# First unit's 47-point result copied across partitions on chip; its row sums on VectorE, its threshold on ACT; token matrix loaded six blocks ahead

## The chip, the cores and the metric

The kernel runs on one core of one Trainium2 chip. The metric is the device time of the program in microseconds, lower is better. The core has five engines that each work through their own list of instructions in order: TensorE (PE, with its weight loads as PEld), VectorE (DVE), ScalarE (ACT), GpSimd (POOL) and SyncE (SP, which here only issues transfers). Transfers are carried out by 16 DMA engines; in this kernel they are issued by SP and by ACT.

## What is computed

```python
def _attn_ref(x, w_r, w_i, b_r, b_i):          # x: 8 x 3008 x 256
    X = np.fft.rfft(x, axis=1)
    Xr, Xi = X.real, X.imag
    Yr = Xr @ w_r - Xi @ w_i + b_r
    Yi = Xr @ w_i + Xi @ w_r + b_i
    Yr = np.sign(Yr) * np.maximum(np.abs(Yr) - 0.01, 0.0)
    Yi = np.sign(Yi) * np.maximum(np.abs(Yi) - 0.01, 0.0)
    return np.fft.irfft(Yr + 1j * Yi, n=3008, axis=1)

def _moe_ref(x, w_tok1, w_tok2, w_ch1, w_ch2):
    h = np.maximum(x.transpose(0, 2, 1) @ w_tok1, 0.0) @ w_tok2
    u = x + h.transpose(0, 2, 1)
    return u + np.maximum(u @ w_ch1, 0.0) @ w_ch2   # 256 -> 1536 -> 256
```

The output is `_moe_ref` of the result of `_attn_ref`. All is float32.

## The kernel before

The transform over 3008 = 47 x 64 points is done with matmuls in two steps: a 47-point step (`dft47`, `stage1`) and a 64-point step (`forward`). The batch of 8 is cut into five units: two of one batch entry (units 0 and 1), three of two. For each unit, `stage1` takes 13 groups of 5 residues each (`NG`, `GS`): a load of `x` with 120 partitions, matmuls with the constant `f1`, an eviction by ACT into a tile `a`, and a store to a scratch tensor `a_d` in DRAM. The next step needs the data with another index on the partitions: it is read back as `a2`, one load for each of 12 pairs `kp` of frequencies. Then, per `kp`: `forward` (matmuls `px`, eviction `xf`, a row sum), `mix` (matmuls `pm` with the channel weights, bias, threshold at 0.01 with DVE), `inverse` (matmuls `pi`, stored to `b_d`), and `tokens` (matmuls `gp` with the transformed token matrix).

Unit 0 is special (`plain`): it runs in `begin`, before anything else can, in float32 without splitting into high and low halves. Beside it, `begin` prepares what all units share. The token matrix `wt1` comes as 13 blocks in float64 words that ACT and DVE turn into float32 (`load_wide`, `narrow`: two ACT and six DVE operations a block); it goes through the 47-point step as well (`prepare_w1`, result in `a_w`), and through a 64-point step (`make_w`). The channel weights `w1` and `w2` are turned into float32 and split.

The loop of `begin` has `NW + KP` passes; in pass n stand one or two groups of `wt1`, `forward` of n, `mix` of n−1, `inverse` of n−3, and from n = `NW` on `make_w` of n−`NW` and `tokens` two passes later. From pass `NC` on the channel weights are prepared (`ahead`). `NC` also decides, before the change, which subtractions of the threshold run on POOL (pairs below 8) and which on DVE. Once `begin` is done, TensorE works through the channel matmuls (`channel`) of one unit while the next unit's transform is woven in.

The order on each engine comes from a scheduler that starts from this program order. Waits follow from the tiles: PSUM has a pool of four banks (`w`) for all matmul results but two. Each DMA counts up one of eight lanes (`DMAHW0` to `DMAHW7`), which are given out in turn to the DMAs of SP and ACT together; a DMA waits until the one before it on its lane has landed. So no more than eight are on their way, and an engine whose next instruction is a DMA stands until that lane is free.

Of the kernel before, what the change touches and what calls it, by code (L numbers as in the profile page):

```python
# [10 lines left out]
F32 = mybir.dt.float32  # L11
# [9 lines left out]
NW, NC = 11, 8  # L21
# [3 lines left out]
GS = 5  # L25
# [93 lines left out]
def tile_kernel(ctx: ExitStack, tc: tile.TileContext, io):  # L119
# [67 lines left out]
    sc = const.tile([128, 16], F32, name="sc")[:, :2]  # L187
# [33 lines left out]
    def sum_diff(x, w, eng, pool):  # L221
        if pool is not None:
            return x
# [10 lines left out]
    def stage1(sd, dst, g, w, pool):  # L234
# [3 lines left out]
        elif dst is a_w:  # L238
            a = pool.tile([120, 2, w], F32, name="a", bufs=2)
        else:  # L240
            t = ("xtl", "xf", "wt", "et", "xtl", "xf", "wt", "et", "xtl")[g % 9]
            a = wk.tile([120, 2, w], F32, tag=t, name="a", bufs=2)
# [11 lines left out]
        rows = dst.rearrange("(i n) k w -> (n k) i w", i=2)  # L254
        (DMA if pool else PUT).dma_start(out=rows[g * 120:g * 120 + n * KH, :, :w], in_=a[:n * KH])

    def dft47(load, dst, w, ahead, eng, pool=None):
# [17 lines left out]
        for g in range(NG):  # L275
# [4 lines left out]
            stage1(sds.pop(g), dst, g, w, pool)  # L280
# [7 lines left out]
    def prepare_w1(pool):  # L288
        tags = ("hl", "o", "early", "hl", "o", "early", "hl", "o", "hl")

        raws = {g: load_raw(io["wt1"][g], 2 * DT, pool) for g in range(3)}

        def load(g):
            return load_wide(io["wt1"][g], 2 * DT, pool, tags[g % 9], raw=raws.pop(g, None)).rearrange("p (i w) -> p i w", i=2)

        return dft47(load, a_w, DT, 3, V, pool)
# [60 lines left out]
    def split_w1(q, t, f):  # L357
        cols = slice(q * 512, (q + 1) * 512)
        split(wc["w1h"][:, t, cols], wc["w1l"][:, t, cols], f, S, V)
# [13 lines left out]
    def parts(u):  # L373
# [6 lines left out]
        def load_unit(g):  # L380
            src = io["x"][bs[0] // 2, g].rearrange("q i (b c) -> q i b c", b=2)
            if plain and g < 12:
                x = wc["x"][g // 6][:, g % 6]
            else:
                x = ld([120, 2, nb, C], "x")
# [11 lines left out]
        def forward(kp, b, a2):  # L397
            pt = bank("px")
            for t in range(2):
                for ab in range(2):  # L400
                    o = (2 * t + ab) * 128
                    PE.matmul(pt[:, o:o + 128], lhsT=a2[:, ab, b, t * 128:(t + 1) * 128], rhs=f2cols(2 * kp + ab), start=True, stop=True)  # L402
            xf = wk.tile([128, 3, 4, 64], F32, tag="xth" if plain else "xf", name="xf", bufs=2)
            S.copy(out=xf[:, 1:3], in_=pt.rearrange("p (q i m) -> p i q m", i=2, m=64))  # L404
            G.tensor_tensor(out=xf[:, 0], in0=xf[:, 1], in1=xf[:, 2], op=ALU.add)  # L405
# [8 lines left out]
        def mix(xt, yh, yl, eng=V):  # L414
# [15 lines left out]
            V.tensor_scalar(out=cl, in0=y, scalar1=LAM, scalar2=-LAM, op0=ALU.min, op1=ALU.max)  # L430
            eng.tensor_tensor(out=yh if plain else y, in0=y, in1=cl, op=ALU.subtract)
# [408 lines left out]
```

## Time and profile before

| | us |
|---|---|
| runs: median (lowest to highest of 3) | 2465.56 (2464.93 to 2467.65) |
| profiled execution, its time | 2465.8 |
| profiled execution, its span | 2464.0 |
| TensorE busy / DVE / ACT / POOL | 2431.6 / 1103.6 / 858.7 / 328.0 |
| first forward matmul (`px`) starts | 42.73 |
| first matmul of the first unit's tokens result (`pu`) starts | 163.88 |

The profile shows one execution. Times in a timeline are microseconds from the start of the span; a row gives the start, the length, the engine, the line of the program, the operation, output <- input, how many, and in brackets how long the engine had been idle and what ended that. `SPq` and `ACTq` are the queues of SP and ACT in which DMAs are issued.

### The profile page before, as it was taken

How to read it: one execution, taken by the hardware profiler on the slowest of the kernel's cores; microseconds unless marked ns; L12 is line 12 of the kernel's file. 1: busy time of each engine (PE TensorE's matmuls, PEld its weight loads, DVE VectorE, ACT ScalarE, POOL GpSimd, SP SyncE). 2: the span in 40 equal slices, each digit the busy share in tenths (PEclk: the TensorE clock that was granted, in tenths of full speed). 3: DMA queues.
4: the chain of work that ended last, by engine and by line, in shares of the span. 5: the costliest groups of instructions: out<-in, count | busy, mean ns of one | idle time of the engine just before them, and what ended most of it. 6: DMA issues, size and time to landing. Idle time of an engine off the chain costs nothing.

```text
span 2464.0 us, 31639 instructions
## 1 busy us (share of the span) xinstructions
PE 2431.6 (99%) x12800; PEld 2116.0 (86%) x12800; DVE 1103.6 (45%) x1734; ACT 858.7 (35%) x1559; POOL 328.0 (13%) x279
## 2 busy tenths in 40 slices
PE   7989999999999999999999999999999999999999
PEld 6768999988888888888888898888888888888887
DVE  5876665455445444433344454434334333232332
ACT  4464444443334343333333343333333222222221
POOL 0200223122223111111111110111111000000000
PEclk9999999999999999999999999999999999999999
DMA  8785334562333453222222363222311122112110
GB/s 250 215 260 155 93 114 140 150 192 84 99 90 97 123 170 91 77 71 88 71 80 80 95 175 105 79 73 82 112 62 41 54 65 63 47 60 78 39 56 18
DMA packets 150484, 252.17 MB, mean 102 GB/s; under 512 B 11009, under 2 KB 104161, under 8 KB 150337
## 3 DMA queue, kind: packets, MB, share of 16 engines
q1 hardware_dynamic: 123825, 199.80, 27.2%
q10 hardware_dynamic: 26512, 50.34, 6.5%
q8 instruction: 101, 1.65, 0.3%
q14 instruction: 46, 0.38, 0.1%
HBM read 162.68 MB, written 87.43 MB: 102 GB/s over the span
## 4 chain that ended last, share of the span: by engine, by line
PE 90%; DMA 3%; issue 3%; DVE 2%; SPq 1%; ACT 0%; POOL 0%; DVEq 0%; ACTq 0%; POOLq 0%
PE ph L178 10%; PE po L179 10%; PE po L178 10%; PE po L180 10%; PE ph L179 10%; PE ph L180 10%; PE pu L679 4%; PE px L402 3%; PE pm L180 2%; PE pm L178 2%; PE pm L179 2%; PE pu L178 2%; PE pu L179 2%; PE pu L180 2%; PE gp L178 2%
## 5 line engine op out<-in xcount | busy, mean ns | idle before, releaser
L718 DVE SCALAR_TENSOR_TENSOR hlo<-ph,hh 128x512 fp32r<-128x512 f32 (+4 forms) x588 | 392.0, 667 | 644.2 <-ACT hh L717 641.3
L717 ACT ACTIVATE hh<-ph 128x512 fp32r<-128x512 f32 (+4 forms) x588 | 340.4, 580 | 816.6 <-PE ph L180 811.5
L178 PE MATMUL ph<-uh,w1h 128*128 128x512 f32 (+4 forms) x1176 | 455.9, 388 | 0.3 <-DVE hlo L718 0.3
L179 PE MATMUL ph<-ul,w1h 128*128 128x512 f32 (+4 forms) x1176 | 449.7, 382 | 0.1
L179 PE MATMUL po<-hlo,w2h 128*128 128x512 f32 (+4 forms) x1176 | 448.2, 381 | 1.6 <-DVE hlo L718 1.6
L180 PE MATMUL ph<-uh,w1l 128*128 128x512 f32 (+4 forms) x1176 | 448.8, 382 | 0.0
L178 PE MATMUL po<-hh,w2h 128*128 128x512 f32 (+4 forms) x1176 | 448.7, 382 | 0.0
L180 PE MATMUL po<-hh,w2l 128*128 128x512 f32 (+4 forms) x1176 | 448.0, 381 | 0.0
L179 PEld LDWEIGHTS po<-hlo,w2h 128*128 128x128 f32 x1176 | 220.9, 188 | 40.7 <-DVE hlo L718 2.3
L180 PEld LDWEIGHTS ph<-uh,w1l 128*128 128x128 f32 x1176 | 221.1, 188 | 39.5
L178 PEld LDWEIGHTS po<-hh,w2h 128*128 128x128 f32 x1176 | 221.0, 188 | 38.6
L180 PEld LDWEIGHTS po<-hh,w2l 128*128 128x128 f32 x1176 | 221.0, 188 | 38.6
L178 PEld LDWEIGHTS ph<-uh,w1h 128*128 128x128 f32 x1176 | 221.5, 188 | 35.6 <-DVE hlo L718 1.2
L179 PEld LDWEIGHTS ph<-ul,w1h 128*128 128x128 f32 x1176 | 221.6, 188 | 34.7 <-DVE ul L688 0.8
L137 DVE TENSOR_TENSOR xtl<-xf,xth 128x768 fp32r<-128x768 f32 x84 | 80.5, 958 | 193.9 <-ACT xth L134 193.7
L405 POOL TENSOR_TENSOR xf<-xf 128x256 f32<-128x256 f32 x96 | 80.7, 841 | 551.3 <-ACT xf L404 550.9
L137 POOL TENSOR_TENSOR yl<-z,yh 128x512 fp32r<-128x512 f32 x72 | 92.7, 1288 | 412.8 <-ACT yh L134 412.8
L178 PE MATMUL pm<-wmh,xth 128*128 128x256 f32 x504 | 144.5, 287 | 0.1
L686 ACT COPY uf<-pu 128x470 f32<-128x470 f32 (+23 forms) x188 | 62.7, 375 | 232.4 <-PE pu L679 232.4
L180 PE MATMUL pm<-wmh,xtl 128*128 128x256 f32 x504 | 142.5, 283 | 0.4 <-DVE xtl L137 0.3
L179 PE MATMUL pm<-wml,xth 128*128 128x256 f32 x504 | 142.4, 283 | 0.0
L679 PEld LDWEIGHTS pu<-g,b 96*128 96x128 f32 x1024 | 130.7, 191 | 3.7 <-issue 0.3
(121 smaller groups left out, 3223.1 us busy)
## 6 DMA issues: line engine op xcount, KB each, us to landing
wt<-wt_d SPq DMA_DIRECT2D x28, 940.0 KB, 5.7
x<-in_x SPq DMA_DIRECT2D x39, 480.0 KB, 4.6
a<-a_d SPq DMA_DIRECT2D x36, 512.0 KB, 3.9
b_d<-bt ACTq DMA_DIRECT2D x36, 512.0 KB, 3.3
out<-o SPq DMA_DIRECT2D x34, 512.0 KB, 2.8
a_d<-a ACTq DMA_DIRECT2D x36, 480.0 KB, 3.5
wt<-wt_d SPq DMA_DIRECT2D x21, 752.0 KB, 5.1
b<-b_d SPq DMA_DIRECT2D x32, 480.0 KB, 6.2
```

The costliest lines, as they stand in the source:

```text
L137: lo_eng.tensor_tensor(out=lo, in0=src, in1=hi.bitcast(F32), op=ALU.subtract)
L178: PE.matmul(out, lhsT=wh, rhs=xh, start=start, stop=False)
L179: PE.matmul(out, lhsT=wh, rhs=xl, start=False, stop=False)
L180: PE.matmul(out, lhsT=wl, rhs=xh, start=False, stop=stop)
L402: PE.matmul(pt[:, o:o + 128], lhsT=a2[:, ab, b, t * 128:(t + 1) * 128], rhs=f2cols(2 * kp + ab), start=True, stop=True)
L405: G.tensor_tensor(out=xf[:, 0], in0=xf[:, 1], in1=xf[:, 2], op=ALU.add)
L679: PE.matmul(pt[:, s * TOKS:(s + 1) * TOKS], lhsT=b2[:, s, cs], rhs=g2[:, 0 if s0 + s == 0 else 1], start=False, stop=s == k - 1)
L686: S.copy(out=ufs[m][:, ct, lo - at:hi - at], in_=pt[:, lo - c0:hi - c0])
L717: S.activation(out=hh, in_=pt, func=AF.Relu)
L718: V.scalar_tensor_tensor(out=hlo, in0=pt, scalar=0.0, in1=hh.bitcast(F32), op0=ALU.max, op1=ALU.subtract)
```

## The change

For unit 0, the DRAM scratch of the 47-point result goes. `a2` is one tile of 128 partitions that holds the whole result (in the place of the later `w1` tile), and each group's eviction is followed by two DMAs from SBUF to SBUF that put 120 rows of 1 KB into 5 partitions of 24 rows each: the cosine half on ACT's queue into partitions from 0 on, the sine half on SP's into partitions from 64 on. `forward` reads `a2` directly.

DVE now adds and subtracts the two halves of each `x` group of unit 0, which halves the matmuls of `stage1` there (two for a group in place of four). The row sum in `forward` of unit 0 moves from POOL to DVE. The threshold of unit 0 becomes relu(y − 0.01) − relu(−y − 0.01): two ACT operations and one subtraction, always on DVE, in place of a DVE minimum and maximum and a subtraction on POOL or DVE. The tiles of `x` for unit 0 take the places of buffers that the narrowing uses later.

The blocks of the token matrix are loaded six ahead (before: three), and narrowed two ahead (before: three). Their stores to `a_w` are issued by ACT (before: SP). `NW` goes from 11 to 8, `NC` from 8 to 12, and every pass takes two groups of the token matrix (before: one and two in turn). The two tiles `w1h` and `w1l` become one, `w1`. The loads of `scale` and `g2` stand ahead of unit 0's groups.

```diff
-NW, NC = 11, 8
+NW, NC = 8, 12
...
-            raw = pool.tile([rows, n, 2], U32, name="raw", bufs=3)
+            raw = pool.tile([rows, n, 2], U32, name="raw", bufs=6)
...
     def sum_diff(x, w, eng, pool):
-        if pool is not None:
+        if pool is not None and w == DT and eng is None:
             return x
...
+                elif not adds:
+                    PE.matmul(pt[:120, o:o + w], lhsT=f1[:, i], rhs=sd[:, i], start=True, stop=True)
                 else:
                     PE.matmul(pt[:120, o:o + w], lhsT=f1[:, i], rhs=sd[:, 0], start=True, stop=False)
                     PE.matmul(pt[:120, o:o + w], lhsT=f1[:, 2 * i], rhs=sd[:, 1], start=False, stop=True)
             S.copy(out=a[:, i0:i0 + each].rearrange("p i w -> p (i w)"), in_=pt[:120])
-        rows = dst.rearrange("(i n) k w -> (n k) i w", i=2)
-        (DMA if pool else PUT).dma_start(out=rows[g * 120:g * 120 + n * KH, :, :w], in_=a[:n * KH])
+        if pool is not None and not adds:
+            for i in range(2):
+                (PUT, DMA)[i].dma_start(out=dst[i * N2 + g * GS:i * N2 + g * GS + n], in_=a[:n * KH, i])
+        else:
+            rows = dst.rearrange("(i n) k w -> (n k) i w", i=2)
+            PUT.dma_start(out=rows[g * 120:g * 120 + n * KH, :, :w], in_=a[:n * KH])
...
-        raws = {g: load_raw(io["wt1"][g], 2 * DT, pool) for g in range(3)}
+        raws = {g: load_raw(io["wt1"][g], 2 * DT, pool) for g in range(6)}
...
+            f = load_wide(None, 2 * DT, pool, tags[g % 9], raw=raws.pop(g)).rearrange("p (i w) -> p i w", i=2)
+            if g + 6 < NG:
+                raws[g + 6] = load_raw(io["wt1"][g + 6], 2 * DT, pool)
+            return f
...
-        return dft47(load, a_w, DT, 3, V, pool)
+        return dft47(load, a_w, DT, 2, None, pool)
...
+                    x = a2[:, 2 * kp + ab, cs] if plain else a2[:, ab, b, cs]
+                    PE.matmul(pt[:, o:o + 128], lhsT=x, rhs=f2cols(2 * kp + ab), start=True, stop=True)
...
-            G.tensor_tensor(out=xf[:, 0], in0=xf[:, 1], in1=xf[:, 2], op=ALU.add)
+            (V if plain else G).tensor_tensor(out=xf[:, 0], in0=xf[:, 1], in1=xf[:, 2], op=ALU.add)
...
-            V.tensor_scalar(out=cl, in0=y, scalar1=LAM, scalar2=-LAM, op0=ALU.min, op1=ALU.max)
-            eng.tensor_tensor(out=yh if plain else y, in0=y, in1=cl, op=ALU.subtract)
-            if not plain:
+            if plain:
+                S.activation(out=cl, in_=y, func=AF.Relu, scale=-1.0, bias=lam)
+                S.activation(out=y, in_=y, func=AF.Relu, bias=lam)
+                V.tensor_tensor(out=yh, in0=y, in1=cl, op=ALU.subtract)
+            else:
+                V.tensor_scalar(out=cl, in0=y, scalar1=LAM, scalar2=-LAM, op0=ALU.min, op1=ALU.max)
+                V.tensor_tensor(out=y, in0=y, in1=cl, op=ALU.subtract)
                 split(yh, yl, y, S, G)
...
-            x = dft47(p.load_unit, p.a, p.w, NG, V, early)
+            a2 = const.tile([128, KH, C], F32, tag="w1", name="a2")
+            x = dft47(p.load_unit, a2, p.w, NG, V, early)
...
-            a2s = {k: p.load_a(k) for k in range(2)}
...
-                for _ in range(2 if n % 2 == 0 else 1):
+                for _ in range(2):
                     next(w1, None)
...
-                    if 0 < n < KP - 1:
-                        a2s[n + 1] = p.load_a(n + 1)
-                    xts[n] = p.forward(n, 0, a2s.pop(n))
+                    xts[n] = p.forward(n, 0, a2)
+                if n == KP - 1:
+                    wc["w1"] = const.tile([128, 2, 2, DF], F32R, tag="w1", name="w1")
```

SP's queue, before, between the loads of the three first blocks of the token matrix (`raw`) and the first store of unit 0's result (`a_d`); `w_r`, `w_i`, `b_r`, `b_i` are the channel-mix weights, `e` a constant of `inverse`:

```order
L164 DMA raw_107<-in_wt1 120x1024 [waits DMAHW7_49]
L164 DMA raw_109<-in_wt1 120x1024 [waits DMAHW0_49]
L164 DMA raw_111<-in_wt1 120x1024 [waits DMAHW1_49]
L340 DMA wf2_113<-in_w_r 128x2x256 [waits DMAHW2_49]
L340 DMA wf2_113<-in_w_i 128x2x256 [waits DMAHW3_49]
L342 DMA bias_74<-in_b_r 128x256 [waits DMAHW4_49]
L342 DMA bias_74<-in_b_i 128x256 [waits DMAHW5_49]
L323 DMA ef_122<-in_e 128x256 [waits DMAHW6_49]
L323 DMA ef_124<-in_e 128x256 [waits DMAHW7_49]
L255 DMA a_d0_83<-a_126 120x2x256 [waits DMAHW0_49,Activation_49]
```

The same place of SP's queue with the change, from the fourth block on:

```order
L164 DMA raw_118<-in_wt1 120x1024 [waits DMAHW3_49]
L164 DMA raw_120<-in_wt1 120x1024 [waits DMAHW5_49]
L164 DMA raw_122<-in_wt1 120x1024 [waits DMAHW6_49]
L349 DMA wf2_125<-in_w_r 128x2x256 [waits DMAHW7_49]
L349 DMA wf2_125<-in_w_i 128x2x256 [waits DMAHW0_49]
L351 DMA bias_74<-in_b_r 128x256 [waits DMAHW1_49]
L351 DMA bias_74<-in_b_i 128x256 [waits DMAHW2_49]
L332 DMA ef_134<-in_e 128x256 [waits DMAHW3_49]
L332 DMA ef_136<-in_e 128x256 [waits DMAHW4_49]
L571 DMA sc_73<-in_scale 128x2 [waits DMAHW5_49]
L572 DMA g2_72<-in_g2 96x2x94 [waits DMAHW6_49]
L258 DMA a2_90<-a_146 5x24x256 [waits DMAHW7_49,Activation_49]
```

Three more blocks, `scale` and `g2` now stand ahead of the first copy, which waits on the lane of `w_r`; the destination has 5 outer rows where the store had 120.

ACT's list at its start with the change; before it held only the evictions (`a<-p1`) here, with no DMA between them:

```order
L255 COPY a_146<-p1_147 120x512 [waits PE_49]
L258 DMA a2_90<-a_146 5x24x256 [waits DMAHW1_49,Activation_49]
L255 COPY a_156<-p1_157 120x512 [waits PE_49]
L255 COPY a_166<-p1_167 120x512 [waits PE_49]
L258 DMA a2_90<-a_156 5x24x256 [waits DMAHW4_49,Activation_49]
L258 DMA a2_90<-a_166 5x24x256 [waits DMAHW0_49,Activation_49]
L255 COPY a_176<-p1_177 120x512 [waits PE_49]
L255 COPY a_186<-p1_187 120x512 [waits PE_49]
```

ACT's third copy has moved behind `w_i`, whose lane (0) it waits for, and the evictions of the fourth group and of all that follow stand behind it.

TensorE's list with the change, between the two first groups of the token matrix (`wide`) and the first forward step (`px`):

```order
L253 MATMUL p1_325<-wide_281,f1_69 120x256 [waits DVE_49,Activation_49]
L254 MATMUL p1_325<-wide_281,f1_69 120x256
L253 MATMUL p1_325<-wide_281,f1_69 120x256
L254 MATMUL p1_325<-wide_281,f1_69 120x256
L418 MATMUL px_332<-f2_71,a2_90 128x128 [waits DMAHW4_49,DMAHW3_49,DMAHW5_49,DMAHW2_49,DMAHW6_49,DMAHW1_49,DMAHW7_49,DMAHW0_49,Activation_49]
L418 MATMUL px_332<-f2_71,a2_90 128x128 x3
L253 MATMUL p1_352<-wide_294,f1_69 120x256 [waits DVE_49,Activation_49]
```

Before, the first `px` waited for one load of `a2`; now it waits on all eight lanes, that is for the last of the 26 copies. It has kept its place behind two groups of the token matrix.

More of the change, by code (lines that the diff above doesn't have):

```diff
@@ L358, in split_w1 @@
         cols = slice(q * 512, (q + 1) * 512)
-        split(wc["w1h"][:, t, cols], wc["w1l"][:, t, cols], f, S, V)
+        split(wc["w1"][:, 0][:, t, cols], wc["w1"][:, 1][:, t, cols], f, S, V)
     def narrow_w2(r, tag="o"):
@@ L381, in load_unit @@
             src = io["x"][bs[0] // 2, g].rearrange("q i (b c) -> q i b c", b=2)
-            if plain and g < 12:
-                x = wc["x"][g // 6][:, g % 6]
+            if not plain:
+                x = ld([120, 2, nb, C], "x")
+            elif g % 2 == 0:
+                tag = ("hl", "o")[g // 2 % 2]
+                x = wk.tile([120, 2, 2, nb, C], F32, tag=tag, name="x", bufs={"o": 3, "hl": 4}[tag])
+                wc["x"] = x[:, 1]
+                x = x[:, 0]
             else:
-                x = ld([120, 2, nb, C], "x")
+                x = wc["x"]
             DMA.dma_start(out=x, in_=src[:, :, bs[0] % 2:bs[0] % 2 + nb])
@@ L412, in forward, with mix @@
             return xh, xl
-        def mix(xt, yh, yl, eng=V):
+        def mix(xt, yh, yl):
             p1, p2 = bank("pm1"), bank("pm2")
```

29 lines of the change are left out of this document (13 added, 16 removed).

## Prediction

> **What bounds the kernel now.** I read the page first (span, busy shares, chain), then a table of windows for the start of the span, then TensorE's waits there, and at last the timeline and the DMA views of the few microseconds that the change touches.
>
> ```profile
> span 2464.0 us, 31639 instructions
> PE 2431.6 (99%) x12800; PEld 2116.0 (86%) x12800; DVE 1103.6 (45%) x1734; ACT 858.7 (35%) x1559; POOL 328.0 (13%) x279
> PE 90%; DMA 3%; issue 3%; DVE 2%; SPq 1%; ACT 0%; POOL 0%; DVEq 0%; ACTq 0%; POOLq 0%
> ```
>
> TensorE is busy 2431.6 of 2464.0 us, so only some 32 us can be won by filling gaps. The windows say where they lie (time, then busy time of PE, PEld, DVE, ACT and POOL, then the granted clock, the DMA engines' busy share and GB/s):
>
> ```profile
> 5.80:35.20 29.40, 28.73 (x120) 23.16 (x120) 12.21 (x24) 13.71 (x27) 0.00 (x0) 1.00 0.99 278
> 35.20:42.70 7.50, 0.00 (x0) 0.00 (x1) 0.79 (x2) 1.66 (x3) 0.00 (x0) 0.64 0.90 231
> 42.70:163.90 121.20, 111.96 (x569) 88.46 (x569) 98.73 (x189) 61.77 (x122) 23.54 (x21) 0.98 0.78 238
> 300.00:400.00 100.00, 100.00 (x634) 95.32 (x634) 56.45 (x104) 43.14 (x81) 22.28 (x19) 1.00 0.38 112
> ```
>
> From 300 us on TensorE has no gap (100.00 of 100). All that the change can move is ahead of that: a start that is DMA-bound (0.99 busy), a hole of 7.5 us, and the loop of the first unit with 121.20 − 111.96 = 9.2 us of gaps. Whatever delays the end of that loop delays the end of the kernel by as much.
>
> ```profile
> 34.60 0.59 PE L252 MATMUL p<-wide,f 120*120 120x256 f32 x2
> 42.73 2.04 PE L402 MATMUL px<-f,a 128*128 128x128 f32 x8 [7.54 <-ACT wide L148]
> 16.16 0.58 SPq L340 DMA_DIRECT2D wf<-in_w_i  x1
> 23.26 11.17 SPq L255 DMA_DIRECT2D a_d<-a  x13
> 37.67 0.90 SPq L394 DMA_DIRECT2D a<-a_d  x2
> ```
>
> The hole ends at 42.73, when the first forward step (L402) gets its operand. The row names ACT, but its real releaser is the load of `a2`: issued at 37.67, and such loads land 5.0 us later (the row of `a<-a_d` below). The 13 stores ahead of it went out only from 23.26 on, although the first evictions were there at 10: SP's queue had the loads of weights in front of them. I call the moment in which the forward steps can start **T0**; it is 42.7 now.
>
> **What the change does to T0.** The stores and loads (13 and 12) give way to 26 copies from SBUF to SBUF, and three more blocks of the token matrix stand ahead of them on SP. Two things have to be priced: when the copies can begin, and how fast they run.
>
> ```profile
> 15.00:20.00 5.00, 5.00 (x25) 4.24 (x24) 0.00 (x0) 1.97 (x6) 0.00 (x0) 1.00 1.02 254
> 20.00:25.00 5.00, 5.00 (x25) 4.23 (x24) 3.34 (x8) 3.48 (x6) 0.00 (x0) 1.00 1.02 232
> 25.00:30.00 5.00, 4.36 (x19) 3.10 (x18) 5.00 (x11) 4.17 (x8) 0.00 (x0) 1.00 1.02 348
> wf<-in_w_r SPq DMA_DIRECT2D x1, 256.0 KB, 10.4
> a<-a_d SPq DMA_DIRECT2D x12, 256.0 KB, 5.0
> a_w<-a SPq DMA_DIRECT2D x1, 192.0 KB, 2.2
> ```
>
> *Begin.* In the new order SP's first copy waits on lane DMAHW7, last used by `w_r`; ACT's third copy waits on lane 0, last used by `w_i`, and behind it ACT's later evictions stand still, so that TensorE, with four PSUM banks, stops after a few groups. `w_i` was issued at 16.16 (`w_r` just before, at about 15.5) and landed some 10.4 us later: 25.9 for `w_r`. Now 3 x 480 KB = 1.47 MB more lie ahead of it, at the 254 and 232 GB/s of the stretch in which these blocks run, 6.1 us. So the copies begin at about 32.0; only ACT's first two are out sooner. Behind SP's copies stand the other seven blocks of the token matrix; nobody needs them before T0. On the same engines `w_i`, two biases, two `e` and `g2` follow, 0.86 MB or 54 KB an engine, 2.5 us.
>
> *Speed.* DMA engines work at 348 / 16 / 1.02 = 21.3 GB/s each with 1 KB packets (row 25:30, mostly the stores that fall away). How many engines carry one copy? A window in which only loads of `x` run tells how a transfer is shared out:
>
> ```profile
> DMA packets 1830, 1.76 MB, mean 252 GB/s; under 512 B 109, under 2 KB 1830, under 8 KB 1830
> x<-in_x SPq DMA_DIRECT2D x8, 240.0 KB, 4.7
> ```
>
> 1830 − 109 = 1721 packets of 1 KB are 7.17 loads of 240 rows, and with each come 109 / 7.17 = 15.2 short packets. I read these as each engine's mark that its part has landed: a load of 120 partitions uses 15 engines, the largest number up to 16 that divides 120. A copy of the change has 120 partitions on its source side but 5x24x256 on its destination: 5 partitions outermost. If engines are dealt whole outer rows, as the 15 suggest, no more than 5 can share it. From 32.0 on, 24 copies are left (13 on SP, 11 on ACT), each 24 packets of 1 KB for each of its engines: 24 x 24 x 1024 B = 0.59 MB an engine, and at 21.3 GB/s **27.7 us**, with the other 11 engines idle.
>
> [...]
>
> So T0 = 32.0 + 2.5 + 27.7 + 2.2 (landing of the last, as the smallest store row) = 64.4, that is **+21.7 us**. The ends: at the whole run's mean rate the copies take longer, at the best seen a little less.
>
> ```profile
> q1 hardware_dynamic: 123825, 199.80, 27.2%
> ```
>
> 199.80 MB in 27.2% of 16 engines' 2464 us are 18.6 GB/s an engine: 31.7 us, 4.0 more. A faster engine than 21.3 shows in no row for 1 KB packets; if 15 engines shared each copy it would be 9.2 us (rival C).
>
> **The other edits.** Ahead of T0 they cost and save nothing, since the copies are the cover. Half of the first stage's matmuls go (26 at 0.43 us, 11 us), but TensorE waits for T0 anyway. The 26 sums and differences on DVE (row L225, 11 us) and the eager preparation of six blocks fall into time in which DVE and ACT idle. If T0 came as early as 40, this work would be late next.
>
> Behind T0 the loop does the same work on TensorE, 112 us with 9.2 us of gaps. What changes there:
>
> ```profile
> L225 DVE TENSOR_TENSOR sd<-x 120x256 f32<-120x256 f32 x4 | 1.7, 425 | 3.4 <-DMA x<-in_x 3.2
> L405 POOL TENSOR_TENSOR xf<-xf 128x256 f32<-128x256 f32 x12 | 11.0, 919 | 65.4 <-ACT xf L404 65.4
> L431 POOL TENSOR_TENSOR held<-z 128x512 f32<-128x512 f32 x8 | 11.3, 1410 | 26.8 <-DVE z L430 26.8
> L431 DVE TENSOR_TENSOR held<-z 128x512 f32<-128x512 f32 x4 | 3.3, 818 | 0.0
> L430 DVE TENSOR_SCALAR z<-z 128x512 f32<-128x512 f32 x12 | 5.0, 419 | 0.1
> L149 ACT ACTIVATE raw<-raw 120x512 f32<-120x512 uint32 x13 | 8.8, 678 | 0.0
> 102.53 0.59 ACTq L450 DMA_DIRECT2D b_d<-bt  x1
> 64.20 1.03 PE L446 MATMUL pi<-held,ef 128*128 128x256 f32 x4
> 72.00 1.03 PE L446 MATMUL pi<-held,ef 128*128 128x256 f32 x4
> ```
>
> DVE gains 12 row sums at about 0.42 (5 us) and 8 subtractions at 0.82 (6.5), and loses 12 thresholds at 0.42 (5) and three blocks prepared before T0 (six operations each, about 3.4 a block, 10): some 4 us less of 98.7. ACT gains 24 thresholds at about 0.68 (16) and 11 stores of the token matrix at 0.59 to issue (6.5), and loses three blocks' 2 x 0.68 (4): 62 becomes 80, plus its old stores. In one pass of the loop with two blocks ACT then has two evictions, two issues, `xf`, two thresholds, `bt`, one issue and on average one block: 1.2 + 1.2 + 0.6 + 1.4 + 0.6 + 0.6 + 1.4 = 7.0 us, against the 7.8 us that TensorE needs (64.20 to 72.00). It fits, barely.
>
> The shorter loop (20 passes instead of 23) moves the token weights forward and puts the channel weights last, where DVE has room. I leave that at nothing, with the whole of the gaps, −9.2, as the best end and one wait of 1.2 us (eviction and store) in each of seven passes, +8, as the worst. What I count are the waits that a lighter DVE and one PSUM user less in a row could end:
>
> ```profile
> PE px L402 <- DVE z L427: 0.9, 1, 0.9
> PE pm L422 <- DVE z L427: 0.5, 1, 0.5
> PE p L251 <- DVE z L427: 0.5, 1, 0.5
> PE pm L422 <- DVE z L429: 0.2, 1, 0.2
> ```
>
> That is **−2.1 us**. The profiled execution took 2465.8 us, 1.8 us around its span, and lies 0.2 over the median of the runs, 2465.56. The sum is 2465.8 + 21.7 − 2.1 = **2485.4 us**.
>
> **Rivals.**
>
> [...]
>
> *C, the copies are shared out over all engines.* Then 2.90 MB take 2.90 / 15 / 21.3 = 9.1 us, T0 = 32.0 + 2.5 + 9.1 + 2.2 = 45.8, +3.1 − 2.1: **2466.8**, not slower. For it speaks that the source has 120 partitions, which take 15 engines; against it that one engine would have to split a destination row. The price turns to a gain if the loop also loses most of its gaps: with −9.2 it is 2459.7. This is also the case in which the change does what it says, a round trip of store and load saved.
>
> *D, ACT becomes the bound of the loop.* On top of the forecast, the seven passes lose 1.2 us each, **2495**, if ACT's 7.0 us grow past 7.8, for example by its stores waiting on lanes. Its two slacks of 0.8 speak against it.
>
> **How the numbers follow.** Forecast 0.52, with its own range of 2475 to 2499 (rates and loop ends together); D 0.09; B 0.10; C 0.29. A measurement of this kernel tells some 0.2%, 4.9 us, from no change. Faster (under 2461) is the part of C with most of the gaps gone: 0.13. Within 0.2% is the rest of C but for 0.02, and the lowest edge of the forecast: 0.14. Slower: 0.73. The range from 2463 to 2502 leaves out C's gains and B's upper half.
>
> **What would show it.** In the changed trace: landing times of the copies of 20 us and more behind their issue or a stretch from about 35 to 62 us with the DMA share near a third (5 of 16) and some 107 GB/s; the first `px` near 64 us; then a loop of about 119 us to the first `pu`. Wrong on the share-out: a DMA share near 0.9 in that stretch and `px` near 46. Wrong on the loop: `px` where I put it, but the first `pu` not 121 us behind it.

## The result, and the profile after

| | before | with the change |
|---|---|---|
| median of 5 runs each, us (lowest to highest) | 2465.56 (2462.70 to 2467.65) | 2491.45 (2489.93 to 2492.48) |
| span of the profiled execution | 2464.0 | 2490.2 |
| first `px` (T0) | 42.73 | 74.99 |
| first `px` to first `pu` | 121.15 | 120.19 |
| first `pu` to the end of the span | 2300.1 | 2295.0 |

The change makes the kernel slower, by a ratio of 1.0103 (95% interval 1.0089 to 1.0118), some 26 us. In the two profiled spans the +26.2 us split into +32.3 ahead of T0, −1.0 in the loop and −5.1 behind it.

The page of the changed kernel: span, busy shares of the engines, and the shares of the chain that ended last.

```profile
span 2490.2 us, 31528 instructions
...
PE 2423.2 (97%) x12748; PEld 2109.3 (85%) x12748; DVE 1107.7 (44%) x1769; ACT 873.3 (35%) x1583; POOL 306.1 (12%) x259
...
PE 89%; DMA 4%; issue 3%; DVE 3%; ACT 1%; SPq 0%; POOL 0%; ACTq 0%; DVEq 0%; POOLq 0%
```

TensorE has 8.4 us less work (2431.6 before, 2423.2 now) and a span that is 26.2 us longer, so its idle time doubled, from 32.4 to 67.0 us. The windows show where (columns as before: time and length, busy time of PE, PEld, DVE, ACT, POOL, then granted clock, DMA share and GB/s).

```profile
20.00:32.00 12.00, 0.00 (x0) 0.00 (x0) 2.62 (x7) 0.00 (x0) 0.00 (x0) 0.50 0.99 234
32.00:45.00 13.00, 5.52 (x16) 4.06 (x16) 4.02 (x10) 2.15 (x4) 0.00 (x0) 0.58 0.56 122
45.00:62.00 17.00, 1.99 (x8) 1.38 (x8) 0.99 (x3) 3.22 (x6) 0.00 (x0) 0.74 0.34 99
62.00:70.00 8.00, 0.96 (x2) 0.80 (x3) 5.29 (x12) 5.98 (x11) 0.00 (x0) 0.50 0.38 105
74.99:195.18 120.19, 112.50 (x570) 89.09 (x569) 95.64 (x201) 75.59 (x146) 1.71 (x1) 0.97 0.69 215
195.18:315.18 120.00, 119.58 (x674) 107.81 (x674) 87.06 (x164) 60.46 (x108) 10.92 (x10) 1.00 0.47 147
```

From 20 to 32 us the DMA engines are full (0.99) and the compute engines do next to nothing. From 45 to 62 us they are a third busy, and still everything waits: that is the stretch of the copies. In it, the view of the DMAs counts packets by size and what was issued:

```profile
DMA packets 1710, 1.68 MB, mean 99 GB/s; under 512 B 66, under 2 KB 1710, under 8 KB 1710
...
a<-a SPq DMA_DIRECT2D x7, 120.0 KB
a<-a ACTq DMA_DIRECT2D x6, 120.0 KB
```

1710 − 66 = 1644 packets of 1 KB are 13.7 copies of 120 rows, with 66 / 13.7 = 4.8 short packets each. Read as one mark for each engine that carries a part, a copy uses **five engines** (a load of 240 rows before: 15.2). 99 GB/s over five engines are 19.8 GB/s each.

The timeline around T0 shows the order of releases: the copies' issue on SP and ACT, ACT's first operation behind its last copy, then TensorE.

```profile
37.21 28.72 SPq L258 DMA_DIRECT2D a<-a  x13
...
60.11 3.86 ACTq L258 DMA_DIRECT2D a<-a  x2
64.02 0.66 ACT L148 ACTIVATE wide<-raw 120x512 f32<-120x512 f32 x1 [4.27 <-DMA a<-a]
...
69.04 1.18 PE L253 MATMUL p<-wide,f 120*120 120x256 f32 x2 [20.83 <-DVE wide L155]
...
74.99 1.13 PE L418 MATMUL px<-f,a 128*128 128x128 f32 x8
```

ACT could not narrow a block (L148) before its last copy was out at 64.0; so DVE could not finish one before 69.0; so the two groups of the token matrix that stand ahead of `px` in TensorE's list ran from 69.04 to 74.99, largely at half clock (0.50 granted up to 73 us, 1.00 from 73.8 to 75). But the copies were not through before that either. The chain of waits gives for some of them the issue and the time to landing:

```profile
40.15 12.84 DMA a<-a
53.07 10.15 DMA a<-a
```

The semaphore updates in the trace, by which a lane counts the landing of its DMA, show the same for the rest: every copy issued from 46 us on lands 9.5 to 10.5 us behind its issue, and the last one, issued by SP at 65.25, at 74.75. So the last copy lands 0.2 us ahead of `px`, and the two groups end with it: either alone would have held `px` until about 75.

TensorE's two longest waits (total, times, longest) are both for what ACT does behind its copies, its evictions and its narrowing:

```profile
PE p L251 <- ACT a L255: 25.3, 2, 23.9
PE p L253 <- DVE wide L155: 20.8, 1, 20.8
```

### The profile page after: what moved, and what is told of

The parts are those of the page before. It is cut to its first block, busy times and chain, and to the rows that moved or that the text cites. A ratio compares the mean times of both kernels' runs of the same rounds, so it can differ in the third digit from the quotient of the medians.

```text
span 2490.2 us, 31528 instructions
## 1 busy us (share of the span) xinstructions
PE 2423.2 (97%) x12748; PEld 2109.3 (85%) x12748; DVE 1107.7 (44%) x1769; ACT 873.3 (35%) x1583; POOL 306.1 (12%) x259
## 4 chain that ended last, share of the span: by engine, by line
PE 89%; DMA 4%; issue 3%; DVE 3%; ACT 1%; SPq 0%; POOL 0%; ACTq 0%; DVEq 0%; POOLq 0%
PE ph L178 10%; PE po L178 10%; PE ph L179 10%; PE po L179 10%; PE po L180 10%; PE ph L180 10%; PE pu L697 4%; PE px L418 3%; PE pm L180 2%; PE pm L178 2%; PE pm L179 2%; PE pu L178 2%; PE pu L179 2%; PE pu L180 2%; PE gp L178 2%
## 5 line engine op out<-in xcount | busy, mean ns | idle before, releaser
L178 PE MATMUL ph<-uh,w 128*128 128x512 f32 (+4 forms) x1176 | 455.5, 387 | 0.1
L179 PE MATMUL ph<-ul,w 128*128 128x512 f32 (+4 forms) x1176 | 449.1, 382 | 0.0
L180 PE MATMUL ph<-uh,w 128*128 128x512 f32 (+4 forms) x1176 | 448.4, 381 | 0.0
L180 PEld LDWEIGHTS ph<-uh,w 128*128 128x128 f32 x1176 | 220.8, 188 | 39.4
L178 PEld LDWEIGHTS ph<-uh,w 128*128 128x128 f32 x1176 | 221.4, 188 | 35.4 <-DVE hlo L736 0.8
L179 PEld LDWEIGHTS ph<-ul,w 128*128 128x128 f32 x1176 | 221.3, 188 | 33.9 <-DVE ul L706 0.2
L421 POOL TENSOR_TENSOR xf<-xf 128x256 f32<-128x256 f32 x84 | 69.7, 830 | 497.9 <-ACT xf L420 487.6
```

The source lines that it names most:

```text
L178: PE.matmul(out, lhsT=wh, rhs=xh, start=start, stop=False)
L179: PE.matmul(out, lhsT=wh, rhs=xl, start=False, stop=False)
L180: PE.matmul(out, lhsT=wl, rhs=xh, start=False, stop=stop)
L421: (V if plain else G).tensor_tensor(out=xf[:, 0], in0=xf[:, 1], in1=xf[:, 2], op=ALU.add)
```

## The experiments

All are the changed kernel with one thing different, unless another kernel is named. Ratios are to the kernel before, run on the same chip beside them; T0 and the loop (first `px` to first `pu`) are from the profiled execution.

| run | median us | ratio (95%) | T0 | loop |
|---|---|---|---|---|
| the change | 2491.45 | 1.0103 (1.0089 to 1.0118) | 74.99 | 120.2 |
| copies undone | 2471.03 | 1.0029 (1.0019 to 1.0039) | 53.99 | 122.8 |
| all copies on SP | 2499.87 | 1.0146 (1.0130 to 1.0161) | 81.14 | 120.9 |
| three blocks ahead | 2495.94 | 1.0125 (1.0108 to 1.0143) | 69.26 | 124.5 |
| all copies on POOL | 2534.26 | 1.0282 (1.0265 to 1.0299) | 120.14 | 115.7 |
| `px` first | 2498.78 | 1.0143 (1.0124 to 1.0161) | 72.00 | 129.0 |
| copies of one partition | 2521.27 (one run) | | 105.92 | 119.5 |
| copies undone, three blocks at first | 2475.36 | 1.0039 (1.0025 to 1.0052) | 47.41 | 126.4 |
| before + row sum and threshold moved | 2473.66 | 1.0038 (1.0023 to 1.0052) | 44.69 | 128.6 |
| row sum and threshold back | 2504.18 | 1.0149 (1.0131 to 1.0166) | 74.11 | 131.5 |
| the same, copies undone | 2476.31 | 1.0036 (1.0025 to 1.0047) | 53.23 | 124.0 |
| the same, copies undone, three blocks at first | 2472.17 | 1.0023 (1.0013 to 1.0033) | 49.12 | 127.1 |
| threshold and row sum on DVE alone | 2488.13 | 1.0087 (1.0073 to 1.0101) | 74.72 | 118.0 |

No version is faster than the kernel before.

### Copies undone

```diff
-            for i in range(2):
-                (PUT, DMA)[i].dma_start(out=dst[i * N2 + g * GS:i * N2 + g * GS + n], in_=a[:n * KH, i])
+            rows = dst.rearrange("(i n) k w -> (n k) i w", i=2)
+            DMA.dma_start(out=rows[g * 120:g * 120 + n * KH, :, :w], in_=a[:n * KH])
...
-            x = dft47(p.load_unit, a2, p.w, NG, V, early)
+            x = dft47(p.load_unit, p.a, p.w, NG, V, early)
...
+            for k in range(KP):
+                DMA.dma_start(out=a2[:, 2 * k:2 * k + 2], in_=p.a[:, 2 * k:2 * k + 2, :C])
```

> The change with one part undone: unit 0's 47-point result goes through DRAM again (13 stores of 120 rows on SP, 12 loads of two frequencies each into the one a2 tile), all else as in the change. Theory (the copies are slow because each has only 5 of the 16 DMA engines): stores begin at about 37 us as the copies do, but use 15 engines, so they are through by about 50, the first load lands 5 us later, ACT is not held by copies and the two groups of the token matrix are done before: first px at 55 to 58 instead of 75.0, time 2491 - 18 = 2473 (2468 to 2478). Rival (the copies cost little, the loss is the queue of weights ahead and the in-order narrowing): px at 68 or later, time above 2483.

It is as the theory said: T0 falls by 21.0 us to 53.99, a little below the 55 to 58 expected, since the stores began at 32.62 and not at 37; the time goes from 1.0103 to 1.0029, 18 us by the ratios. Its windows over the stores and the loads:

```profile
32.00:40.00 8.00, 3.61 (x9) 2.79 (x10) 6.97 (x16) 5.70 (x10) 0.00 (x0) 0.50 0.98 309
40.00:50.00 10.00, 2.71 (x13) 1.97 (x11) 4.56 (x9) 1.17 (x2) 0.00 (x0) 0.84 0.94 261
```

Moving the bytes twice, out to DRAM and back, in a stretch that runs at 261 to 309 GB/s, beats moving them once at 99. Seven tenths of the loss are the copies (18 of 25 us by the ratios). What is left are 11.3 us of T0 over the kernel before, given back in part behind the loop.

### How a copy is shared out: copies of one partition

```diff
-                (PUT, DMA)[i].dma_start(out=dst[i * N2 + g * GS:i * N2 + g * GS + n], in_=a[:n * KH, i])
+                for r in range(n):
+                    at = i * N2 + g * GS + r
+                    (PUT, DMA)[i].dma_start(out=dst[at:at + 1], in_=a[r * KH:(r + 1) * KH, i])
```

> The change with each copy cut into copies of one destination partition of 24 rows (24 KB, 5 or 4 for each old copy, 122 in all). It asks how a copy is shared out. If whole destination partitions are dealt to engines: one mark (short packet) per copy, px near 85 to 95 since 61 issues per queue at 0.6 to 0.75 us take 40 us and more, 2500 to 2512 us. If the largest number up to 16 that divides the outermost count of both sides, with 24 rows as outermost here: 12 marks per copy, a DMA share above 0.34 between 45 and 62, and px near 70 to 80.

The DMA view between 45 and 62 us:

```profile
DMA packets 1260, 0.86 MB, mean 51 GB/s; under 512 B 420, under 2 KB 1260, under 8 KB 1260
...
a<-a SPq DMA_DIRECT2D x18, 24.0 KB
a<-a ACTq DMA_DIRECT2D x17, 24.0 KB
```

840 rows of 1 KB are 35 copies of 24, with 420 / 35 = **12.0** short packets each: read as before, 24 rows into one destination partition are carried by 12 engines. So engines aren't dealt by destination partition, as I had put it in the prediction; that would give 1 here and falls. The second wording of the expectation gives 12 here, 5 for the copies of the change and 15 for the loads of `x`, and the counts 12.0, 4.8 and 15.2 agree with it; no more than these three shapes were counted. The rest of both expectations missed: T0 came at 105.92, since with small copies the issue is the limit, 64 of them in 61.43 us on SP:

```profile
33.20 61.43 SPq L260 DMA_DIRECT2D a<-a  x64
```

That is 0.96 us an issue, where 0.60 to 0.75 had been expected; 9.3 of the 61.43 us SP waited for lanes. The DMA share meanwhile is 0.22 (45 to 60 us), so the engines are not the limit.

### One queue for the copies: SP, then POOL

```diff
-                (PUT, DMA)[i].dma_start(out=dst[i * N2 + g * GS:i * N2 + g * GS + n], in_=a[:n * KH, i])
+                DMA.dma_start(out=dst[i * N2 + g * GS:i * N2 + g * GS + n], in_=a[:n * KH, i])
```

> The change with all 26 copies issued by SP, none by ACT; the same bytes over the same five engines, but ACT's evictions and narrowing are no longer behind copies. Theory (5 engines set the end of the copies, and what ACT does late adds the two groups of the token matrix behind that end): copies end at 70 to 73, since the two early copies of ACT are lost, the DMA share stays at a third from 38 to 70, the two groups run before px, px at 70 to 73 instead of 75.0, time 2486 to 2490. Rival (ACT standing in front of its lanes is the main cost): px at 55 or earlier, time under 2475.

And with all 26 copies issued by POOL's queue, their source, destination and 1 KB pieces unchanged:

> [...] Theory (few engines per copy, always the same five): if the engines differ from copy to copy, the DMA share has no stretch near a third, the copies run beside the loads from 10 us on and px comes at 45 to 52, time 2462 to 2470; if POOL uses the same five engines, the copies still start early but end at about 40 to 50. Rival B (writing into five neighbouring partitions is slow whatever engine does it): a copy stays at 2 us or more, 26 x 2 us behind the first eviction at 10: px at 60 or later, time above 2476.

Both missed. With all copies on SP, ACT issues none, the two groups are done by 50 us, and TensorE's waits name the copies alone as what `px` waits for:

```profile
PE px L418 <- DMA a<-a: 31.4, 1, 31.4
```

Two rows of the chain of waits (issue, time to landing) and two windows show where the time went:

```profile
47.73 5.14 DMA a_w<-a
69.78 11.26 DMA a<-a
```

```profile
50.00:60.00 10.00, 0.00 (x0) 0.00 (x0) 0.00 (x0) 1.93 (x4) 0.00 (x0) 0.71 0.32 75
66.00:70.00 4.00, 0.00 (x0) 0.00 (x0) 0.00 (x0) 0.00 (x0) 0.00 (x0) 0.50 0.34 100
```

SP issues no copy from 45.2 to 52.89: its next one needs the lane of a store that ACT issued at 47.73 and that landed 5.14 us later. The last copy goes out at 69.78, while the theory had the copies end at 70 to 73, and it lands 11.26 us later, with block loads issued behind it from 71.09 on. At first few bytes move (75 GB/s from 50 to 60 us, the standstill included); from 66 to 70 us one queue moves 100 GB/s at a DMA share of 0.34, as much as the two queues of the change. So the run doesn't show that a second queue is worth anything, nor what a free ACT wins: a wait for a lane stands in between.

On POOL's queue another limit took over. The DMA view between 82 and 118 us gives the time from issue to landing last, and POOL's timeline the issues:

```profile
a<-a POOLq DMA_DIRECT2D x11, 120.0 KB, 5.4
```

```profile
28.79 0.73 POOL L258 DMA_DIRECT2D a<-a  x1 [8.37 <-issue]
33.21 0.64 POOL L258 DMA_DIRECT2D a<-a  x1 [3.69 <-issue]
```

Most of POOL's issues stand 1.5 to 9 us apart, and a copy lands 5.4 us later. That says nothing on five engines or fifteen; that the time lies in rival B's range (above 2476) is no proof of it. Why POOL pauses between issues stays open.

### Fewer blocks ahead

```diff
-            raw = pool.tile([rows, n, 2], U32, name="raw", bufs=6)
+            raw = pool.tile([rows, n, 2], U32, name="raw", bufs=3)
...
-        raws = {g: load_raw(io["wt1"][g], 2 * DT, pool) for g in range(6)}
+        raws = {g: load_raw(io["wt1"][g], 2 * DT, pool) for g in range(3)}
...
-            if g + 6 < NG:
-                raws[g + 6] = load_raw(io["wt1"][g + 6], 2 * DT, pool)
+            if g + 3 < NG:
+                raws[g + 3] = load_raw(io["wt1"][g + 3], 2 * DT, pool)
```

> The change with the token matrix loaded three blocks ahead as before (3 instead of 6 blocks stand ahead of the copies on SP). Theory: the copies begin 3 x 2.4 = 7 us earlier, at about 31, and take their 31 us all the same, ACT narrows only three blocks behind its last copy: px at 66 to 69, time 2482 to 2486. Rival (the copies would be hidden behind the loads, so that when they begin does not matter): time within 2 us of 2491.

T0 came earlier by 5.7 us, close to what was expected (69.26 for 66 to 69), but the time didn't: the median is 4.5 us above the change's (the intervals overlap), and both expectations missed. TensorE's timeline names the reason, and SP's where it lies:

```profile
78.74 1.18 PE L253 MATMUL p<-wide,f 120*120 120x256 f32 x2 [6.62 <-DVE wide L155]
```

```profile
60.91 5.54 SPq L164 DMA_DIRECT2D raw<-in_wt  x3
```

The fourth block's load goes out at 60.91, behind SP's 13 copies, so the loop starts with three blocks and TensorE then waits three times for narrowing, 7.3 us in all and 6.62 of them here: 124.5 us for 120.2. The next run mends that, with the copies undone: three blocks at first, the next three behind the first two loads of `a2`.

```diff
-        raws = {g: load_raw(io["wt1"][g], 2 * DT, pool) for g in range(6)}
+        raws = {g: load_raw(io["wt1"][g], 2 * DT, pool) for g in range(3)}
+
+        def more():
+            raws.update({g: load_raw(io["wt1"][g], 2 * DT, pool) for g in range(3, 6)})
...
+            for k in range(2):
+                DMA.dma_start(out=a2[:, 2 * k:2 * k + 2], in_=p.a[:, 2 * k:2 * k + 2, :C])
+            wc["more"]()
+            for k in range(2, KP):
+                DMA.dma_start(out=a2[:, 2 * k:2 * k + 2], in_=p.a[:, 2 * k:2 * k + 2, :C])
```

> The copies go back to stores into DRAM (13, on SP) and loads (12), and only blocks 0 to 2 of the token matrix are loaded ahead of unit 0's groups, blocks 3 to 5 behind the first two loads of the 47-point result. All else as in the change. Theory (the loss is the wait for T0, set by the copies and by what stands ahead of them on SP; the rest of the change is worth a few microseconds): the stores begin near 24, first px at 43 to 47, px to first pu about 120 to 123, 2458 to 2464 us. Rival (the three blocks ahead cost nothing, or the loop needs six blocks at hand): px near 54 as with the copies alone undone, or px near 45 but the loop 5 us longer and more, 2468 to 2472.

T0 is near where the theory put it (47.41 for 43 to 47); the loop is as long as the rival had it (126.4), and the time is above both. 6.6 us won at T0 against the run with the copies undone are more than lost behind it: +3.6 in the loop and +5.5 after the first `pu` (2301.8 for 2296.3), in the profiled executions. The medians stand 4.3 us apart, with intervals that overlap.

### `px` ahead of the two groups

```diff
+                if n < KP and n == 0:
+                    xts[n] = p.forward(n, 0, a2)
...
-                if n < KP:
+                if 0 < n < KP:
```

> The change with the first forward step written ahead of the first two groups of the token matrix, so that TensorE has px next when the copies are through. Theory (T0 is set by the copies, the 5.9 us of the two groups only stand between them and px, but the narrowing of the blocks on DVE is behind by then and takes the 5.9 us back): px at 68 to 71, first pu 192 to 196, 2488 to 2493 us. Rival (the two groups ahead of px cost their 5.9 us): px at 69, first pu 189, 2485 us.

Both theories missed. Three rows of TensorE's timeline show what happens:

```profile
72.00 2.05 PE L418 MATMUL px<-f,a 128*128 128x128 f32 x8 [24.70 <-DMA a<-a]
73.85 1.06 PE L253 MATMUL p<-wide,f 120*120 120x256 f32 x2
...
82.13 1.06 PE L418 MATMUL px<-f,a 128*128 128x128 f32 x8
```

`px` comes 3.0 us sooner, but the two groups, their first matmuls at 1.06 us for two where the later ones take 0.59, now run behind it and count in the loop; the second `px` starts at 82.13. The loop is 8.8 us longer: the 6 us of the groups and another 2.8 that I can't place. Both expectations took it that only the two groups stood between the copies and `px`. Here nothing stands between, and `px` waits for the copies until 72.00: the last one goes out at 63.23 and lands at 71.76, both sooner than in the change. So the order on TensorE wins nothing at T0; the copies set it.

### Row sum and threshold, alone on the kernel before

```diff
-            G.tensor_tensor(out=xf[:, 0], in0=xf[:, 1], in1=xf[:, 2], op=ALU.add)
+            (V if plain else G).tensor_tensor(out=xf[:, 0], in0=xf[:, 1], in1=xf[:, 2], op=ALU.add)
...
-            V.tensor_scalar(out=cl, in0=y, scalar1=LAM, scalar2=-LAM, op0=ALU.min, op1=ALU.max)
-            eng.tensor_tensor(out=yh if plain else y, in0=y, in1=cl, op=ALU.subtract)
+            if plain:
+                S.activation(out=cl, in_=y, func=AF.Relu, scale=-1.0, bias=lam)
+                S.activation(out=y, in_=y, func=AF.Relu, bias=lam)
+                V.tensor_tensor(out=yh, in0=y, in1=cl, op=ALU.subtract)
...
```

> The kernel before with the row sum of unit 0 on DVE and its threshold as two ACT operations and one DVE subtraction, nothing else of the change. Theory (my term for the loop: the waits on DVE go, ACT has room): px stays at 42.7, px to first pu 118 to 121 us, 2462 to 2466 us. Rival D (ACT becomes the bound of the loop, 24 operations of 0.68 us and no relief): first pu 5 us later and more, 2470 and up.

Rival D's times hold here: 9 us slower by the medians. (The profiled execution is the slowest of its runs, so its loop of 128.6 us overstates it.) ACT's timeline in that loop:

```profile
66.58 0.71 ACT L432 ACTIVATE z<-z,sc 128x512 f32<-128x512 f32 x1
69.42 0.67 ACT L148 ACTIVATE wide<-raw 120x512 f32<-120x512 f32 x1 [2.13 <-DMA raw<-in_wt]
70.00 0.71 ACT L433 ACTIVATE z<-z,sc 128x512 f32<-128x512 f32 x1
```

Its waits for blocks in the loop, and behind them those of the kernel before:

```profile
ACT wide L148 <- DMA raw<-in_wt: 15.6, 8, 4.9
```

```profile
ACT wide L148 <- DMA raw<-in_wt: 18.4, 8, 5.8
```

Between the two halves of one threshold stands the narrowing of a block that hasn't landed, and ACT waits with the second half behind it. ACT isn't full (75.7 of 128.6 us); it is blocked, in order, eight times in the loop. It was so before as well, but then no threshold stood in its line. That the 9 us are these waits is argued and not shown: one place is seen, and the run moves the row sum too. I took from this that six blocks ahead must cure it, since in the loop of the change ACT's longest wait is another:

```profile
ACT z L447 <- DVE z L445: 12.3, 10, 2.0
```

No wait for a block of the token matrix is among its first ten there.

### Row sum and threshold taken back, in the change

The same diff turned round, POOL taking the row sum and the subtractions of pairs below 8 again; in three settings.

> The change with the row sum back on POOL and the threshold back as a DVE minimum and maximum and a subtraction (POOL for pairs below 8, DVE from there), all else as in the change. Theory from the run with the threshold alone (it cost 9 us there because ACT's threshold stood behind narrowing that waited for a block of the token matrix; with six blocks loaded ahead ACT waits for none in the loop): no gain, 2487 to 2495 us, px to first pu 119 to 122. Rival (two more ACT operations in the chain from pm to pi cost by themselves, wherever ACT stands): about 9 us faster than the change, 2480 to 2484, px to first pu 112 to 115.

> The copies undone (13 stores on SP to DRAM, 12 loads) and the row sum and threshold back on POOL and DVE as well; left of the change are the halved matmuls of the first stage, the six blocks loaded ahead, the new order of passes and the stores of the token matrix on ACT. Beside it stands the run with the copies alone undone, 2471.0. Theory (threshold costs only where ACT waits for blocks; there ACT waited 14.5 us for blocks, most of it ahead of px): 2467 to 2472 us. Rival (it costs by itself): 2460 to 2464, faster than the kernel before.

> As the run with three blocks ahead of unit 0's groups and the copies undone (2475.4), with the row sum and the threshold back on POOL and DVE. Theory (there ACT's threshold again stood behind narrowing that waited for blocks, which gave back the earlier px): px near 47, px to first pu 117 to 121, 2462 to 2468 us. Rival (blocks 3 to 5 arriving later starve the narrowing itself, whatever ACT does): px near 47, px to first pu 125 and more, 2472 to 2477.

The first contradicts both theories: it isn't equal to the change, and not faster, but 11 us **slower** (1.0149 for 1.0103). TensorE has a new wait:

```profile
PE pm L438 <- POOL xf L421: 8.2, 1, 8.2
```

POOL's timeline, the chain of waits at that place, and the groups by line tell where it is from:

```profile
76.68 11.70 POOL L421 TENSOR_TENSOR xf<-xf 128x256 f32<-128x256 f32 x2 [76.24 <-ACT xf L420]
94.42 1.66 POOL L447 TENSOR_TENSOR held<-z 128x512 f32<-128x512 f32 x1 [6.04 <-DVE z L446]
```

```profile
76.68 11.03 POOL xf L421
```

```profile
L421 POOL TENSOR_TENSOR xf<-xf 128x256 f32<-128x256 f32 x12 | 20.5, 1715 | 94.4 <-ACT xf L420 94.4
```

Two row sums took 11.70 us, 11.03 of them the first; the twelve have a mean of 1715 ns, where the kernel before had 919. DVE's timeline over the same microseconds:

```profile
76.79 0.68 DVE L155 TENSOR_TENSOR wide<-wide 120x512 f32<-120x512 f32 x1
...
86.43 0.68 DVE L155 TENSOR_TENSOR wide<-wide 120x512 f32<-120x512 f32 x1
89.86 0.69 DVE L443 TENSOR_TENSOR z<-pm,bias 128x512 f32<-128x512 f32 x1 [2.75 <-PE pm L438]
```

The rows between show no gap: DVE works back to back, narrowing blocks and three times splitting channel-mix weights, until 87.11, the end of the row at 86.43; then it waits for TensorE. POOL's first sum starts while DVE is busy, lasts through 21 DVE instructions and is through at 87.71, 0.6 us after DVE stops. With six blocks at hand and T0 this late, narrowing has no pause of its own. That DVE holds the sum up is read from these times; by what way, no run shows.

The other two runs don't separate from their partners: 1.0036 for 1.0029 with the copies undone (2476.3, above both expectations), 1.0023 for 1.0039 with three blocks at first. The last met its rival, with a loop of 127.1 us: that points to the supply of blocks, not to ACT's threshold. With the copies undone, no row sum on POOL takes longer than 1.2 us, though one subtraction there takes 4.80 us where the others take 1.3 to 1.7:

```profile
92.74 4.80 POOL L447 TENSOR_TENSOR held<-z 128x512 f32<-128x512 f32 x1 [6.31 <-DVE z L446]
```

### No POOL, no threshold on ACT

Minimum and maximum, subtraction and row sum of unit 0 all on DVE.

```diff
-            if plain:
-                S.activation(out=cl, in_=y, func=AF.Relu, scale=-1.0, bias=lam)
-                S.activation(out=y, in_=y, func=AF.Relu, bias=lam)
-                V.tensor_tensor(out=yh, in0=y, in1=cl, op=ALU.subtract)
-            else:
-                V.tensor_scalar(out=cl, in0=y, scalar1=LAM, scalar2=-LAM, op0=ALU.min, op1=ALU.max)
-                V.tensor_tensor(out=y, in0=y, in1=cl, op=ALU.subtract)
+            V.tensor_scalar(out=cl, in0=y, scalar1=LAM, scalar2=-LAM, op0=ALU.min, op1=ALU.max)
+            eng.tensor_tensor(out=yh if plain else y, in0=y, in1=cl, op=ALU.subtract)
+            if not plain:
                 split(yh, yl, y, S, G)
...
-                    p.mix(xts.pop(k), ys[k], None)
+                    p.mix(xts.pop(k), ys[k], None, V)
```

> The change with the threshold back as a minimum and maximum and a subtraction, all 24 on DVE, and the row sum on DVE as in the change: unit 0 has no operation on POOL, and none of the threshold on ACT. It stands between the change (2491.5) and the change with threshold and row sum undone (2504.2), where one row sum on POOL took 11.7 us while DVE narrowed blocks back to back. Theory (the 12.7 us were POOL's operations, kept out while DVE runs without a gap, not the relief of DVE by ACT): 2490 to 2495 us, px to first pu 119 to 123. Rival (what the threshold on ACT wins is DVE's time, 12 operations of 0.42 us and the order behind them): 2499 to 2505, px to first pu 127 and more.

The theory holds, with time and loop a little below its ranges (2488.1 and 118.0). The windows of the two loops, first the one with POOL, then the one without:

```profile
74.11:205.61 131.50, 113.14 (x568) 88.03 (x568) 100.52 (x192) 60.52 (x121) 38.33 (x21) 0.96 0.64 197
```

```profile
74.72:192.69 117.97, 111.56 (x568) 87.65 (x568) 97.94 (x211) 60.71 (x121) 1.27 (x1) 0.99 0.70 216
```

Taking 20 operations from POOL makes the loop 13.5 us shorter and the time 15 us by the ratios, though DVE does 19 operations more, in less busy time. And the threshold on ACT is worth nothing in the change: with it 1.0103, without it 1.0087, intervals that overlap. So of the two moves, the one off POOL was needed, with six blocks ahead and T0 as late as the copies make it (with the copies undone, above, it made no measurable difference); the one to ACT was not.

## Why the prediction was right or wrong

The direction, the main mechanism (copies on five engines hold T0) and most of the size were right: 2485.4 was forecast in a range of 2463 to 2502, and 2491.45 measured. Of the profiled difference, +26.2, the sum had +19.6; its terms were off by +10.6, +1.1 and −5.1. That the total came so close is in part luck: the −5.1, which I hadn't forecast, hides half of the miss at T0.

**T0, begin.** 34.5 was forecast; SP's first copy went out at 37.21. `w_i` and what followed it came 2.7 us later than my rate for the blocks gave. In the two runs in which ACT issues no copies, SP's queue was at this place at 32.62 (copies undone) and 31.52 (all copies on SP). So ACT's early copies are the likely reason; by what way isn't shown.

**T0, speed.** Five engines: shown by 4.8 marks a copy, by 99 GB/s at a DMA share of 0.34 (107 and near a third were named as signs), and supported by T0 falling 21.0 us when the copies are undone. My reason for the five, whole outer rows of the destination, was wrong: it doesn't fit the 12.0 marks of the copies of one partition. What was mis-sized is the time that the copies take on them: from 37.21 to the last landing at 74.75 they took 37.5 us, for 29.9 in the sum. These +7.6 are most of the +10.6. On average the 24 landings came 1.38 us apart where I had 1.15, that is 17.8 GB/s an engine for 21.3, a rate taken from stores. And the last copy's landing I took at 2.2 us, from a store with little ahead of it; here each copy landed some 10 us behind its issue, with up to eight on the way. The last four landings also share the DMA engines with the block loads that SP issues from 68.02 on. I had these loads at no cost ("nobody needs them before T0"); what they cost isn't measured.

**T0, the other edits.** I wrote that "the eager preparation of six blocks" would "fall into time in which DVE and ACT idle", at no cost. At T0 that came true, but by luck. DVE and ACT idled, but were not free to work: ACT's narrowing stood behind its last copy, until 64.02, and the two groups ahead of `px` ran from 69.04 to 74.99. They cost at most 0.2 us only because the last copy landed no sooner than 74.75; with copies as fast as forecast they would have stood in the way. Both facts stood in the order of instructions shown ahead of the prediction: ACT's evictions behind its copies, and `px` behind the two groups. I had used the first for the copies alone.

**The loop.** −2.1 was forecast, −1.0 measured, but that is luck: a balance that I hadn't seen. I priced the moves by busy time (4 us less on DVE, POOL free). The runs show other sizes: with the row sum and the subtractions left on POOL the loop is 131.5 us long, with one sum of 11.03 us there beside a DVE that the eager blocks leave without gaps; with all of them on DVE it is 118.0. That is what their move avoids.

**Behind the loop** I had nothing; −5.1 came. In the 120 us after the first `pu` TensorE is busy 119.58 us, before the change 117.28:

```profile
163.88:283.88 120.00, 117.28 (x656) 104.22 (x657) 87.61 (x166) 60.34 (x109) 10.29 (x9) 1.00 0.52 159
```

That is 2.3 of the 5.1. Over all runs this part lies between 2294 and 2303 us, and I didn't find what sets it.

**Rivals.** *B*, slow writes into neighbouring partitions, and its part of the range rest on nothing that a run shows; what was seen of the copies is 99 GB/s from 45 to 62 us, 19.8 for each of five engines. *C* falls with the five engines. *D* does not hold in the change (the threshold on ACT costs nothing measurable); its time, by the way, should have been 2493.8 (2485.4 + 7 x 1.2). On the kernel before, the threshold on ACT and the row sum on DVE do cost time, but not in the way I gave: ACT wasn't too busy (75.7 of 128.6 us), and it is seen standing behind blocks that hadn't landed.

## What to carry to other kernels

Before a round trip through DRAM is replaced by a copy on chip, find out how many DMA engines carry a copy of its shape: here the bytes moved once, at 4.8 marks a copy and a DMA share of 0.34, lost some 18 us to the way out and back at a share of 0.94 to 0.98. Work is free in a wait only if its engine can get at it (here ACT's narrowing stood behind its last copy until 64.02), so look at what stands ahead of it in that engine's line, a DMA that waits for its lane among it. Price the last landing with the transfers that are ahead of it, not with a row of one that had few: here each copy needed some 10 us. And preparing further ahead can turn an engine's gaps into one long stretch, as it did here beside a late T0: then look at the engines that work beside it: here one sum on POOL took 11.03 us beside a DVE without gaps, and 0.73 elsewhere.

## What was not expected of the hardware

- A copy of 24 rows of 1 KB into one partition leaves 12.0 marks, one of 120 rows into five partitions 4.8, which I read as 12 engines and 5.
- With up to eight copies on the way on five engines, a copy landed some 10 us behind its issue, though landings came only 1.38 us apart. One queue moved as much as two (100 GB/s from 66 to 70 us with all copies on SP, 99 in the change).
- A POOL sum that takes 0.7 us elsewhere (0.73 at 150.82 in the same run) took 11.03 us beside a DVE without gaps. In the same run a DVE operation of usually 0.42 us took 1.50 beside a subtraction on POOL (94.42 to 96.08).

```profile
94.85 1.50 DVE L151 TENSOR_SCALAR wide<-raw 120x512 uint32<-120x512 uint32 x1
```
